# Top-k attention and a Fourier mixer on one core: the order of VectorE's top-k passes

## The chip, the cores and the metric

The kernel runs on one core of one Trainium2 chip. A core has five engines with a queue of instructions each, which run in order: TensorE (PE; its weight loads are listed apart as PEld), VectorE (DVE), ScalarE (ACT), GpSimd (POOL) and SyncE (SP), which here issues nearly all DMAs. They wait for one another, and for DMAs, through semaphores. The metric is the device time of one execution in microseconds; shown times are medians of several runs.

## What is computed

Two blocks follow one another. The first is attention in which each query keeps its 32 largest scores; the second mixes tokens and channels by a Fourier transform and puts an MLP behind it.

```python
def _attn_ref(q, k, v):                       # each (8, 8, 576, 64): batch, head, token, head_dim
    scores = scale * np.matmul(q, k.transpose(0, 1, 3, 2))
    kth = np.partition(scores, -top_k, axis=-1)[..., -top_k:-top_k + 1]      # top_k = 32
    scores = np.where(scores >= kth, scores, -1000000000.0)
    scores = scores - np.max(scores, axis=-1, keepdims=True)
    attn = np.exp(scores)
    attn = attn / (np.sum(attn, axis=-1, keepdims=True) + 1e-09)
    return np.matmul(attn, v)

def _moe_ref(x, w_ch1, w_ch2):                # x (8, 576, 512), weights 512 x 2048 and 2048 x 512
    mixed = np.real(np.fft.fft(np.fft.fft(x, axis=1), axis=2))
    u = x + mixed
    un = (u - mean(u)) / np.sqrt(var(u) + 1e-06)
    return u + np.maximum(un @ w_ch1, 0.0) @ w_ch2
```

The heads of a batch, side by side, are the second block's `x`. All is fp32.

## The kernel before

**Tiles.** Heads are taken in pairs, four pairs to a batch. The 576 queries of a pair of heads make nine tiles: four row blocks of 128 for each head, and one tile with the last 64 rows of both. So a batch has 36 tiles and the kernel 288, numbered 0 to 287. A tile is a matrix of 128 queries by 576 scores in the buffer `S` (six of them).

**Top-k on VectorE.** `top_ops` (L407) makes a tile's list of passes. A pass reads 576 scores per row. MAX8 (L425) writes the eight largest into `m`; MATCH_REPLACE8 (L427) writes a copy into `wk` in which these eight are replaced by a very small number. Four rounds of MAX8 with three MATCH_REPLACE8 between them leave the 32 largest in `m`, seven passes in all. The first round reads `S`, the others `wk`. A pass needs the one before it of its own tile: MATCH_REPLACE8 the eight values, the next MAX8 the changed copy. The program has a semaphore wait on VectorE itself for that, except at MAX8 on `S`.

A step `i` of the main loop (L1498) holds the last three passes of tile i, `first` (MAX8, MATCH_REPLACE8, MAX8), and the first four of tile i + 1, `second` (MAX8 on `S`, MATCH_REPLACE8, MAX8, MATCH_REPLACE8). L1611 to L1617 lay them down in turns. After the last pass of `first` the step puts in an integer shift on a weight chunk (`shift`, L200), in batch 0 alone. Behind the passes come small operations where there are some (`late_now` and the "dve" list): the reciprocal of the softmax sums (L591), the normalisation of a finished piece of `x` (L608, L615, from PSUM), statistics (L844), additions of finished products (L1008, L1121).

**What hangs on a tile's last pass.** The 1st and the 32nd of `m` become, on GpSimd, two biases `nt` (`bounds`, L434). ScalarE then makes `wk` from `S` with a steep relu (`mask`, L448), GpSimd subtracts it from `S` (L451), and ScalarE takes the exponential with the row sums (`expo`, L459). In batches 0 and 1 and for the last pair TensorE transposes the result (L527) and ScalarE copies it to `PT`. For the others (`by_dma`) ScalarE splits the words into two planes in `wk` (L472), SyncE sends them to DRAM (L485) and brings them back transposed (L506). TensorE multiplies `PT` with `v` (`attend`, L564). `wk` has three buffers for pairs of tiles and one for the tile of tails; one is free again when its planes are sent, or its transposes done.

**Where `S` comes from.** In step i TensorE makes the scores of tile i + 3 (L401, L386, the last 64 keys in L371), and ScalarE copies them to `S` (L404, L393, L375). ScalarE's queue has, in each step, the mask and the planes of earlier tiles first and these copies behind them.

**The rest of a step.** All queues are written in program order by a planner: it lays the transform of a finished batch (TensorE L755, L812, L816; its folds on GpSimd, or on VectorE for the first and the last batch) and the MLP's units (L966 hidden layer with the relu on ScalarE at L970; L993, L1032 and the products L1163 of the second layer) between the attention of the next batch. The last batch's MLP comes when no attention is left. Nothing is moved while it runs; an engine that comes to an instruction whose input is missing stands still.

Of the kernel before, what the change touches and what calls it, by code (L numbers as in the profile page):

```python
# [73 lines left out]
def kernel(  # L74
# [332 lines left out]
    def top_ops(i, rounds):  # L407

        if not 0 <= i < N:
            return []  # L410
        if i not in Wk:
            e = items[i][2]
            if e != 1:

                if e is None:
                    Wp[i] = attp.tile([P, 1, S], F32, name=f"wk_{i}", tag="W1", bufs=1)
                else:
                    Wp[i] = attp.tile([P, 2, S], F32, name=f"wk_{i}", tag="W", bufs=3)
            Wk[i] = Wp[i - 1][:, 1, :] if e == 1 else Wp[i][:, 0, :]
            M8[i] = small.tile([P, TOPK], F32, name=f"m8_{i}", tag="m8", bufs=5)  # L420
        w, m, s = Wk[i], M8[i], Ssb[i]
        ops = []
        for r in rounds:
            src, m8 = s if r == 0 else w, m[:, 8 * r:8 * r + 8]
            ops.append(lambda src=src, m8=m8: nc.vector.max(out=m8, in_=src))  # L425
            if r < TOPK // 8 - 1:
                ops.append(lambda src=src, m8=m8: nc.vector.match_replace(w, m8, src, NEG))  # L427
        return ops
# [955 lines left out]
    for b in range(B):  # L1384
        end = PER_BATCH * (b + 1) - 1
        last = b == B - 1
        first, soon = b == 0, b == 1
# [91 lines left out]
    def run(i, where):  # L1479
        for fn in plan.pop((i, where), []):  # L1480
            fn()
# [16 lines left out]
    while i < N + 5 or plan or queue or sums:  # L1498
# [111 lines left out]
                load_v(pair_of + 1)  # L1610
        first, second = top_ops(i, (2, 3)), top_ops(i + 1, (0, 1))  # L1611
        for n in range(max(len(first), len(second))):
            for ops in (first, second):
                if n < len(ops):
                    ops[n]()
                if ops is first and n == len(first) - 1:
                    run(i, "shift")  # L1617
# [56 lines left out]
```

## Time and profile before

| what | us |
|---|---|
| median of 3 runs (1851.18 to 1857.1) | 1854.34 |
| span of the profiled execution, first to last instruction | 1848.4 |
| TensorE busy (share of the span) | 1686.1 (91%) |
| VectorE busy | 1581.0 (86%) |
| ScalarE busy | 1294.9 (70%) |
| GpSimd busy | 919.5 (50%) |
| 864 MAX8 on `wk`, L425: busy, mean of one | 626.5, 0.749 |
| 288 MAX8 on `S`, L425 | 213.7, 0.742 |
| 576 MATCH_REPLACE8 on `wk`, L427 | 427.6, 0.742 |
| 288 MATCH_REPLACE8 on `S`, L427 | 213.6, 0.742 |

The span is one execution, the one that was profiled; the median is of other runs, timed without a profile. Top-k passes run from 10 us to 1641 us; what follows is the last batch's transform and MLP. Times in the timeline are microseconds from the span's start. Busy time is the union of the recorded lengths of an engine's instructions. A row of the waits names the waiting engine, tile and line, what it waited for, the total in us, how often and the longest. The chain of waits follows the work that ended last back from the end, at each step to what released it.

### The profile page before, as it was taken

The numbers are of one execution on the slowest core, as the hardware profiler recorded it, in microseconds if no ns is written. First come the engines' busy times: TensorE is split into PE (matmuls) and PEld (weight loads), VectorE is DVE, ScalarE is ACT, GpSimd is POOL, SyncE is SP. The second block draws the span as 40 slices with busy tenths as digits, with TensorE's granted clock in tenths as the row PEclk, the third lists the DMA queues.
The fourth block names the chain that finished last, engine by engine and source line by source line (L and its number), as shares of the span: only waits on it lengthen the run. The fifth ranks groups of instructions, "written<-read, shape, count | busy, mean of one in ns | idle before, by whom it ended". The sixth has DMA issues, their size and how long they took to land.

```text
span 1848.4 us, 26992 instructions
## 1 busy us (share of the span) xinstructions
PE 1686.1 (91%) x8134; PEld 1084.1 (59%) x8134; DVE 1581.0 (86%) x3301; ACT 1294.9 (70%) x3104; POOL 919.5 (50%) x1286
## 2 busy tenths in 40 slices
PE   5676699899898998999999999999999999999998
PEld 3344465374555655667565655666566756686677
DVE  7999989999899999999999999999999899944010
ACT  6878659687788778877787778777887678642100
POOL 4768744556634466356543565356634654350012
PEclk8878899899899999999999999999999999999999
DMA  5334016752558855577566855595566845520051
GB/s 168 107 92 118 20 44 178 189 137 59 127 135 200 214 133 131 134 207 179 117 149 166 222 127 127 137 249 145 137 144 181 199 104 140 152 80 7 6 174 57
DMA packets 513504, 249.16 MB, mean 135 GB/s; under 512 B 398288, under 2 KB 502352, under 8 KB 513360
## 3 DMA queue, kind: packets, MB, share of 16 engines
q1 hardware_dynamic: 511440, 243.04, 51.2%
q0 software_dynamic: 1152, 4.19, 0.7%
q8 instruction: 65, 1.06, 0.2%
q14 instruction: 79, 0.65, 0.1%
q10 hardware_dynamic: 768, 0.21, 0.0%
HBM read 93.63 MB, written 84.74 MB: 96 GB/s over the span
## 4 chain that ended last, share of the span: by engine, by line
PE 45%; DVE 27%; POOL 9%; issue 8%; ACT 7%; DMA 3%; SPq 0%; POOLq 0%; DVEq 0%; ACTq 0%
PE hp L966 16%; DVE wk L427 12%; DVE m L425 12%; PE cp L993 5%; PE o L564 5%; POOL wk L451 4%; PE sp L401 3%; PE cw L1163 3%; PE cv L1163 2%; ACT wk L448 2%; PE yp L755 2%; POOL fg L651 2%; PE cp L1032 2%; PE mp L816 1%; PE sp_t L371 1%
## 5 line engine op out<-in xcount | busy, mean ns | idle before, releaser
L451 POOL TENSOR_TENSOR wk<-S,wk 128x576 f32<-128x576 f32 x288 | 407.6, 1415 | 503.2 <-ACT wk L448 503.1
L425 DVE MAX8 m<-wk 128x8 f32<-128x576 f32 x864 | 626.5, 749 | 6.1
L966 PE MATMUL hp<-unT,w 128*128 128x256 f32 (+1 forms) x2048 | 525.1, 408 | 2.9 <-ACT hT L970 2.1
L966 PEld LDWEIGHTS hp<-unT,w 128*128 128x128 f32 x2048 | 379.5, 191 | 106.7 <-issue 9.9
L427 DVE MATCH_REPLACE8 wk<-m,wk 128x576 f32<-128x576 f32 x576 | 427.6, 742 | 0.0
L472 ACT COPY wk<-S 128x576 uint16<-128x576 uint16 x468 | 289.6, 670 | 0.0
L448 ACT ACTIVATE wk<-S,nt 128x576 f32<-128x576 f32 x288 | 223.5, 776 | 85.4 <-POOL nt L434 84.0
L993 PE MATMUL cp<-w,hT 128*128 128x512 f32 x512 | 232.6, 594 | 0.0
L970 ACT ACTIVATE hT<-hp 128x320 f32<-128x320 f32 (+1 forms) x256 | 103.7, 412 | 179.9 <-PE hp L966 178.2
L425 DVE MAX8 m<-S 128x8 f32<-128x576 f32 x288 | 213.7, 742 | 10.3 <-ACT S L375 10.2
L564 PE MATMUL o<-PT,v 128*64 128x256 f32 (+3 forms) x1440 | 198.7, 421 | 22.0 <-DMA PT<-planes 13.0
L427 DVE MATCH_REPLACE8 wk<-m,S 128x576 f32<-128x576 f32 x288 | 213.6, 742 | 0.0
L459 ACT ACTIVATE S<-wk,nt 128x576 f32<-128x576 f32 x234 | 184.3, 788 | 28.3 <-POOL wk L451 26.8
L401 PE MATMUL sp<-kT,qT 64*128 64x512 f32 (+1 forms) x528 | 168.9, 669 | 9.3 <-ACT means L1357 5.7
L564 PEld LDWEIGHTS o<-PT,v 128*64 128x64 f32 x1440 | 116.0, 155 | 97.8 <-issue 34.5
L404 ACT COPY S<-sp 128x512 f32<-128x512 f32 (+1 forms) x264 | 141.8, 588 | 32.5 <-PE sp L401 31.4
L993 PEld LDWEIGHTS cp<-w,hT 128*128 128x128 f32 x512 | 93.1, 191 | 89.2 <-issue 88.1
L1108 POOL TENSOR_TENSOR hT<-hT 128x512 f32<-128x512 f32 x64 | 81.2, 1275 | 117.8 <-ACT hT L970 87.9
L434 POOL TENSOR_TENSOR nt<-m,cc 128x2 f32<-128x2 f32 x288 | 59.9, 208 | 156.6 <-DVE m L425 154.3
L1163 PE MATMUL cw<-w,hT 128*128 128x256 f32 x448 | 104.9, 384 | 12.6 <-ACT ct L1133 10.2
L371 PEld LDWEIGHTS sp_t<-kt,qT 128*128 128x128 f32 x320 | 51.1, 194 | 102.3 <-issue 68.0
L1163 PEld LDWEIGHTS cw<-w,hT 128*128 128x128 f32 x448 | 82.6, 190 | 28.4 <-ACT ct L1133 12.6
(161 smaller groups left out, 2141.8 us busy)
## 6 DMA issues: line engine op xcount, KB each, us to landing
planes<-wk SPq DMA_DIRECT2D x208, 288.0 KB, 2.8
w<-w_parts SPq DMA_DIRECT2D x82, 512.0 KB, 5.0
space<-in_moe_w_ch_dram SPq DMA_DIRECT2D x32, 512.0 KB, 3.7
nat<-in_q_dram SPq DMA_DIRECT2D x128, 64.0 KB, 2.3
v<-in_v_dram SPq DMA_DIRECT2D x64, 128.0 KB, 3.0
out_dram<-x SPq DMA_DIRECT2D x32, 256.0 KB, 2.8
nat<-in_k_dram SPq DMA_DIRECT2D x62, 128.0 KB, 3.2
planes<-wk SPq DMA_DIRECT2D x52, 144.0 KB, 2.7
```

Source lines behind the costliest of these rows:

```text
L401: nc.tensor.matmul(sp[r], lhsT=qT[hd, q_cols], rhs=kT[hd, :], start=True, stop=True)
L404: nc.scalar.copy(out=s_t[r, keys], in_=sp[r])
L425: ops.append(lambda src=src, m8=m8: nc.vector.max(out=m8, in_=src))
L427: ops.append(lambda src=src, m8=m8: nc.vector.match_replace(w, m8, src, NEG))
L448: nc.scalar.activation(out=w, in_=Ssb[i], func=AF.Relu, scale=-FAR, bias=Nt[i][:, 1:2])
L451: nc.gpsimd.tensor_tensor(out=w, in0=Ssb[i], in1=w, op=ALU.subtract)
L459: nc.scalar.activation(out=Ssb[i] if by_dma(i) else w, in_=w, func=AF.Exp, bias=Nt.pop(i)[:, 0:1], accum_out=den_t[pair % 3][:, c:c + 1],)
L472: nc.scalar.copy(out=words[:, half, :], in_=src[:, half, :])
L564: nc.tensor.matmul(o[D * e:D * (e + 1), c0:c1], lhsT=vv[:, c, e, :], rhs=pt[:, NF if c == NF else (NF + 1) * e + c, c0:c1], start=(c == 0) ...
L966: nc.tensor.matmul(hp[:, 0:w], lhsT=w1[:, dt, P * it:P * (it + 1)], rhs=unT[:, dt, 0:w], start=(dt == 0), stop=(dt == NDT - 1),)
L993: nc.tensor.matmul(cp, lhsT=hT[:, it, P * n:P * (n + 1)], rhs=w2[:, it, :], start=(it == 0), stop=(it == NIT - 1),)
L1163: nc.tensor.matmul(dst, lhsT=h()[a][:, kc, :], rhs=rhs_of(kc), start=start and kc == 0, stop=kc == NK - 1, skip_group_check=True,)
```

## The change

The two lists of passes of a step are laid down in the other turn, the newer tile's first.

```diff
         first, second = top_ops(i, (2, 3)), top_ops(i + 1, (0, 1))
         for n in range(max(len(first), len(second))):
-            for ops in (first, second):
+            for ops in (second, first):
                 if n < len(ops):
                     ops[n]()
                 if ops is first and n == len(first) - 1:
                     run(i, "shift")
```

With F1 to F3 for the passes of `first` and S1 to S4 for those of `second`, VectorE's order in a step was, and becomes (the small operations stand behind the last pass in both):

```
before:  F1 S1 F2 S2 F3 (shift) S3 S4
after:   S1 F1 S2 F2 S3 F3 (shift) S4
```

F1 belongs to the tile of the S1 to S4 one step before. Tile 0's first four passes stand ahead of the loop, and the last tile's step has no `second`. Nothing else in the program is changed.

## The prediction

> **What bounds the kernel now.** The names first. In one step VectorE runs seven passes over 576 keys: F1, F2, F3 finish the older tile (MAX8, MATCH_REPLACE8, MAX8), S1 to S4 begin the newer one (MAX8 on `S`, MATCH_REPLACE8, MAX8, MATCH_REPLACE8). A MATCH_REPLACE8 shows as two rows, a short MATCH_VALUE_LOAD and the pass. I read VectorE's timeline first, one step without other work in it; columns are start, length, line and operation:
>
> ```profile
> 1156.08 0.74 DVE L427 MATCH_REPLACE8 wk<-m,wk 128x576 f32<-128x576 f32 x1
> 1156.85 0.76 DVE L425 MAX8 m<-wk 128x8 f32<-128x576 f32 x1
> 1157.53 0.74 DVE L425 MAX8 m<-S 128x8 f32<-128x576 f32 x1
> 1158.19 0.07 DVE L427 MATCH_VALUE_LOAD wk<-m,wk 128x8 f32 x1
> 1158.25 0.74 DVE L427 MATCH_REPLACE8 wk<-m,wk 128x576 f32<-128x576 f32 x1
> 1158.91 0.08 DVE L427 MATCH_VALUE_LOAD wk<-m,S 128x8 f32 x1
> 1158.98 0.74 DVE L427 MATCH_REPLACE8 wk<-m,S 128x576 f32<-128x576 f32 x1
> 1159.64 1.41 DVE L425 MAX8 m<-wk 128x8 f32<-128x576 f32 x2
> 1161.08 0.09 DVE L427 MATCH_VALUE_LOAD wk<-m,wk 128x8 f32 x1
> 1161.16 0.74 DVE L427 MATCH_REPLACE8 wk<-m,wk 128x576 f32<-128x576 f32 x1
> ```
>
> Read start to start, not by length. A pass that follows a pass of the other tile starts 0.66 to 0.67 us after it (1157.53 to 1158.19, 1158.25 to 1158.91, 1158.98 to 1159.64), which is before the 0.74 us of its forerunner are over. A pass that follows its own tile's starts later: F1 behind the S4 before it 1156.85 - 1156.08 = 0.77, and S4's load behind S3, which began 1159.64 + 0.67 = 1160.31, also 0.77. The reader sees two holds of 0.11 us per step.
>
> Then who waits for whom, VectorE up to the end of its top-k work (0 to 1640 us) and ScalarE in the second 200 us of the dense middle, and the chain of waits from 499 to 812 us; last the busy time by engine in two stretches (length, then PE, its weight loads, DVE, ACT, POOL, the granted clock, DMA share, GB/s):
>
> ```profile
> DVE x L608 <- PE tpx L604: 23.3, 10, 5.5
> DVE m L425 <- ACT S L375: 10.2, 7, 2.2
> DVE rd L591 <- ACT rd L590: 8.6, 6, 4.2
> ...
> DVE wk L427 <- DMA planes<-wk: 4.0, 2, 2.0
> ```
> ```profile
> ACT wk L448 <- POOL nt L434: 28.4, 17, 3.8
> ```
> ```profile
> by line: DVE wk L427 39.8%; DVE m L425 37.0%; issue 11.6%; DVE st L844 1.9%; ACT wk L472 1.9%; DVE x L608 1.2%; ACT wk L448 1.0%; POOL wk L451 0.9%; POOL hT L1108 0.8%; DVE x L1054 0.6%; DVE mv L845 0.6%; DVE x L615 0.6%; POOL nt L434 0.4%;
> ```
> ```profile
> 440.00:640.00 200.00, 182.34 (x873) 113.42 (x872) 188.58 (x390) 154.08 (x367) 102.00 (x149) 0.95 0.64 159
> 840.00:1040.00 200.00, 193.73 (x957) 123.69 (x955) 190.28 (x397) 156.07 (x373) 103.86 (x155) 1.00 0.65 161
> ```
>
> VectorE hardly ever waits: some 70 us in 1640, by the whole list. So where the chain lies on it, a shorter step is a shorter kernel. The chain in order of time has it there in batch 0 (9.5 to 194 us, but for excursions) and from 499 to 812 us, where L427, L425 and VectorE's small work are over four fifths; ScalarE waits there for the thresholds (17 times, 28.4 us), so TensorE is late for VectorE's sake. From 255 to 446 us and from 812 us on the chain is TensorE, GpSimd and ScalarE, but for stints of 3 to 8 steps, and TensorE is idle only 6 us of 200.
>
> **The change, part by part.** The build moves VectorE's rows alone: the order on TensorE, ScalarE, GpSimd and SyncE, DMA issues included, is the same, and so are all counts. The order becomes S1 F1 S2 F2 S3 F3 S4, then S1 of the next tile.
>
> *The holds.* No pass follows its own tile's any more. The new step, each gap from the row of an equal pair above: S1 to F1 0.67 (MAX8 to MAX8 of the other tile, F3 to S3), F1 to S2's load 0.66, its pass 0.06, F2's load 0.66, pass 0.07, S3 0.66, F3 0.67, S4's load 0.66, pass 0.06, next S1 0.66: 4.83 us. The old step is S1 at 1152.45 to S1 at 1157.53, 5.08. A pure step saves 0.25: two holds of 0.11 and 0.01 to 0.02 in each of two neighbours. Where a small operation (a normalisation, statistics, a late addition) stands between S4 and F1, only the hold at S3 and S4 goes: 0.11 + 0.02 = 0.13.
>
> The Trainium skill speaks against this: "VectorE: DVE Perf Modes", section "The DRAIN you can't avoid", holds that the next operation never starts before the pipeline is empty and that a semaphore between chained operations costs nothing extra, measured on eight copies. By it the saving would be 0 and the time, with F3 later, 1856. The rows above disagree, 0.66 against 0.77, and they decide.
>
> *The thresholds.* F3 goes from fifth to sixth place: 0.66 us later in its step, and with it `nt` (L434) on GpSimd, the mask (L448) on ScalarE, the subtraction (L451), and all that ScalarE has queued behind the mask: the copies of `S` for later tiles, relu evictions, the planes. It is paid once each time the chain leaves VectorE through F3, not in each step. Behind the mask lie 4 us of slack in the middle case of batches 4 to 6 (start of L448 minus end of F3, paired by tile), 0.3 to 2 in batch 2's second half.
>
> *The waits.* S1's wait for the `S` copies moves one place forward, S2's wait for a free `wk` buffer too; F1 or F2, and so F3, are now queued behind them. In most steps nothing is waited for: `S` is ready 7 to 9 us before S1 in the middle case. Where it is late, or the buffer is, F3 comes later than before, relative to that event. From a late S1 to the end of the F3 n steps on it was 5.08 n + 2.86 us (1157.53 to 1159.64 + 0.75) and becomes 4.83 n + 4.19 (0.67 + 0.66 + 0.06 + 0.66 + 0.07 + 0.66 + 0.67 + 0.74): 1.33 - 0.25 n more. From a late S2 it was 0.07 + 0.66 + 0.75 = 1.48 and becomes 2.86: 1.38 - 0.25 n. So a stretch between two such waits gains only if it has more than five steps.
>
> *The sum.* Batch 0 up to 194 us: 31 steps, 24 of them pure: 24 x 0.25 + 7 x 0.13 = 6.9, less 0.66 at the exit: 6.2 us. 499 to 812 us: 58 steps, 32 pure: 8.0 + 3.4 = 11.4, less 0.66: 10.7 us. Batch 1 (chain on TensorE): 0, between -1 and +4. Batches 4 to 7: stints of 3 and 7.5 steps, 1.38 - 0.25 x 3 = 0.6 lost and 0.25 x 7.5 - 1.38 = 0.5 won; I take 0 for each batch, with -3 (half of its 6 us of idle TensorE filled) and +1.5 (lost at two waits) as bounds. The tail after 1640 us is MLP on TensorE: 0. Together 16.9 us: the span of 1848.4 becomes 1831.5. The median of the runs, 1854.34, is 5.9 us above the span; I keep that difference: 1837.4, said as 1837.
>
> **Rivals.**
> 1. *TensorE takes it over.* For: TensorE is 97% busy from 840 us on and 91% already in 440 to 640. Then the 10.7 us are eaten by the first TensorE-bound stretch, batch 0's 6.2 remain: 1848. Against: ScalarE's 28.4 us of waits for thresholds, and TensorE idle 17.7 of 200 us there.
> 2. *More than counted.* VectorE saves 81 x 0.25 + 65 x 0.13 = 29 us in batches 4 to 7 as well, and half of TensorE's idle time closes: 3 us a batch, and 4 in batch 1: 1837 - 16 = 1821. Against: `S` comes within 0.3 us of S1 once or twice in each of these batches already, so VectorE will wait there.
> 3. *Slower: the old tile stuck behind the new one.* One mechanism, in batches 4 to 7 (145 steps): a faster VectorE runs into S1's wait at L425, F1 to F3 stand behind it, thresholds come later, ScalarE, whose queue holds the next `S` copies behind the mask, delivers them later still. Price 1.33 - 0.25 n per wait at intervals of n steps. At n = 3, 48 waits x 0.58 = +28 and the time 1865; it eats the 17 us won elsewhere from about n = 3.6. For: the wait moved is a true one. Against: in 0 to 1640 us VectorE waited for `S` 7 times, for anything 38 times in 288 steps, and where `S` is late the masks lag F3 by 4.7 to 11 us already.
> 4. *The change does not do what it says*: the hold belongs to something else, or a pass two places behind its own tile's is held as well. Then no gain and 2 x 0.66 lost: 1856. Against: F1 to F2 and S1 to S2 are two places apart today and run at 0.66.
>
> **How the numbers follow.** Forecast 0.57 (own range 1825 to 1845: batches 4 to 7 at -3 each, or at +1.5 each and three more exits at 0.66), rival 1 0.13, rival 2 0.15, rival 3 0.10, rival 4 0.05. What a measurement can tell from no change is 0.3%, 5.6 us: faster is below 1848.8, slower above 1859.9. Faster: the forecast, rival 2 and half of rival 1: 0.79; the same: the other half, rival 4 and the mild end of rival 3: 0.13; slower: 0.08. The range 1821 to 1851 takes in rivals 1 and 2 and leaves out what lies beyond.
>
> **What would show it.** Right: MATCH_REPLACE8 to MAX8 and MAX8 to load at 0.66 us everywhere, S1 to S1 at 4.83 in pure steps; S1 of tile 36 about 8 us earlier, and of tile 140 about 17; TensorE's busy time the same. ScalarE's waits for `nt` shrink between 499 and 812 us, and VectorE's own waits grow after 812. Wrong: 0.77 still there (rival 4); batches 4 to 7 longer than 201 us with L425 <- `S` at the head of VectorE's waits (rival 3); 499 to 812 not shorter although its steps are (rival 1).

## The result and the profile after

| | before | changed |
|---|---|---|
| median of the runs on the same chip (4 each), us | 1855.37 (1851.18 to 1857.1) | 1843.7 (1843.09 to 1844.21) |
| span of the profiled execution, us | 1848.4 | 1841.7 |

The ratio is 0.994 with a 95% interval of 0.9926 to 0.9954: faster by 0.6%, beyond the 0.3% that can be told from no change, but 6.7 us short of the 1837 forecast. The same kernel run 12 times more, beside 35 runs of the kernel before, gave 0.9955 (0.9937 to 0.9974). So the gain is 8 to 11 us where 16.9 were counted.

First the page of the changed kernel: the span, the busy time of the engines and the groups of top-k passes (busy time and mean ns of one; the last column is the engine's idle time before them and what ended most of it).

```profile
span 1841.7 us, 26992 instructions
PE 1683.0 (91%) x8134; PEld 1082.6 (59%) x8134; DVE 1540.8 (84%) x3301; ACT 1295.2 (70%) x3104; POOL 919.1 (50%) x1286
L425 DVE MAX8 m<-wk 128x8 f32<-128x576 f32 x864 | 618.5, 742 | 0.1
L425 DVE MAX8 m<-S 128x8 f32<-128x576 f32 x288 | 214.8, 746 | 18.5 <-ACT S L375 17.5
```

VectorE's busy time fell by 40.2 us (1581.0 to 1540.8), the span by 6.7. The mean of a MAX8 on `wk` hardly moved (749 to 742 ns): a hold lies between two starts, not in a length. One step of the changed kernel in VectorE's timeline, F1 to the next F1 (columns: start, length, line and operation):

```profile
1143.14 0.74 DVE L425 MAX8 m<-wk 128x8 f32<-128x576 f32 x1
1143.80 0.07 DVE L427 MATCH_VALUE_LOAD wk<-m,S 128x8 f32 x1
1143.86 0.74 DVE L427 MATCH_REPLACE8 wk<-m,S 128x576 f32<-128x576 f32 x1
1144.52 0.08 DVE L427 MATCH_VALUE_LOAD wk<-m,wk 128x8 f32 x1
1144.59 0.74 DVE L427 MATCH_REPLACE8 wk<-m,wk 128x576 f32<-128x576 f32 x1
1145.25 1.41 DVE L425 MAX8 m<-wk 128x8 f32<-128x576 f32 x2
1146.57 0.07 DVE L427 MATCH_VALUE_LOAD wk<-m,wk 128x8 f32 x1
1146.63 0.74 DVE L427 MATCH_REPLACE8 wk<-m,wk 128x576 f32<-128x576 f32 x1
1147.29 0.75 DVE L425 MAX8 m<-S 128x8 f32<-128x576 f32 x1
1147.96 0.74 DVE L425 MAX8 m<-wk 128x8 f32<-128x576 f32 x1
```

Every gap is 0.66 to 0.67 us and the step takes 1147.96 - 1143.14 = 4.82 us. Where S4 stood 0.77 behind S3, it now stands 1.32 behind the start of the pair S3 and F3 (1145.25 to 1146.57), two gaps of 0.66. Over all steps of batches 1 to 7 the median from S1 to S1 went from 5.08 or 5.09 to 4.82 or 4.83.

What became of it shows in the waits. VectorE, 0 to 1640 us (tile and line, what it waited for, total us, times, longest), then ScalarE's wait for the thresholds from 499 to 812 us, in the changed kernel, and last that wait in the kernel before:

```profile
DVE x L608 <- PE tpx L604: 32.0, 19, 6.2
DVE wk L427 <- DMA planes<-wk: 22.1, 4, 8.2
DVE rd L591 <- ACT rd L590: 21.4, 13, 3.6
DVE m L425 <- ACT S L375: 17.5, 11, 3.4
```
```profile
ACT wk L448 <- POOL nt L434: 23.5, 20, 4.0
```
```profile
ACT wk L448 <- POOL nt L434: 28.8, 22, 4.0
```

All four of VectorE's rows grew, from 46 us to 93 together; its waits up to 1640 us add to some 121 us, 68 before. ScalarE's wait for `nt` in that stretch shrank from 28.8 us to 23.5. The chain of waits by line, 499 to 812 us, has changed its head:

```profile
by line: PE hp L966 11.1%; issue 5.6%; DVE m L425 5.6%; POOL wk L451 4.6%; DVE wk L427 4.4%; PE o L564 4.2%; ACT wk L448 3.6%; ACT wk L472 3.4%; PE sp L401 2.4%; PE cw L1163 2.4%; ACT S L459 2.4%; PE cp L1032 2.3%; POOL fg L651 1.9%; PE cp 
```

L427 and L425 were 77% of it before and are 10% now; the MLP's matmuls on TensorE lead. Where the time was won is read best on TensorE, which runs the same instructions in the same order in all kernels here. The time between the same marked matmuls, in us:

```
stretch (times of before)          14-236      236-445     445-812     812-1640
before                             221.6       209.2       367.2       828.0
changed                            219.9       211.1       357.7       830.3
mean of the old order (profiles)   222.4 (4)   212.4 (7)   366.7 (6)   830.6 (7)
mean of the new order (profiles)   220.3 (6)   212.4 (7)   359.8 (8)   833.7 (6)
```

The last two rows take every profile of this study whose edit leaves that stretch in the one order or the other, without those with shifts or conversion left out where it is batch 0, and without the kernel that changes a wait in the last stretch. The kernel that moves F3 alone (below) counts as old, since its step is as long. In 445 to 812 us the two orders do not overlap (365.1 to 368.6 against 357.7 to 361.9). In 14 to 236 us they overlap a little (221.6 to 224.1 against 219.4 to 222.0), in 236 to 445 and 812 to 1640 us clearly.

Whole spans of single profiles decide nothing at this size: the changed kernel's second profile had a span of 1854.7 us, 13 us more than the first, and 35 runs of the kernel before lie between 1850.4 and 1864.7. Nor need a profiled execution be typical: that of the second profile was the slowest of its kernel's 12 runs, and so were, among theirs, those of four kernels below (batches 2 and 3 alone, batches 4 to 7 alone, shift behind the step, no shifts in the new order). So totals are compared by ratios over many runs below, and profiles by stretches.

### The profile page after: what moved, and what is told of

The parts are those of the page before. It is cut to its first block, busy times and chain, and to the rows that moved or that the text cites. A ratio compares the mean times of both kernels' runs of the same rounds, so it can differ in the third digit from the quotient of the medians.

```text
span 1841.7 us, 26992 instructions
## 1 busy us (share of the span) xinstructions
PE 1683.0 (91%) x8134; PEld 1082.6 (59%) x8134; DVE 1540.8 (84%) x3301; ACT 1295.2 (70%) x3104; POOL 919.1 (50%) x1286
## 4 chain that ended last, share of the span: by engine, by line
PE 45%; POOL 8%; ACT 6%; issue 5%; DMA 2%; DVE 2%; SPq 0%; POOLq 0%; DVEq 0%; ACTq 0%
PE hp L966 18%; PE o L564 4%; PE cw L1163 4%; PE cp L993 4%; POOL wk L451 4%; PE sp L401 3%; PE cv L1163 3%; PE cp L1032 2%; ACT wk L448 2%; POOL fg L651 2%; DMA PT<-planes 1%; PE mp L816 1%; PE sp_t L371 1%; ACT wk L472 1%; DVE m L425 1%
## 5 line engine op out<-in xcount | busy, mean ns | idle before, releaser
L425 DVE MAX8 m<-wk 128x8 f32<-128x576 f32 x864 | 618.5, 742 | 0.1
L427 DVE MATCH_REPLACE8 wk<-m,wk 128x576 f32<-128x576 f32 x576 | 425.9, 739 | 0.0
L425 DVE MAX8 m<-S 128x8 f32<-128x576 f32 x288 | 214.8, 746 | 18.5 <-ACT S L375 17.5
L564 PE MATMUL o<-PT,v 128*64 128x256 f32 (+3 forms) x1440 | 199.5, 422 | 24.5 <-DMA PT<-planes 19.7
L427 DVE MATCH_REPLACE8 wk<-m,S 128x576 f32<-128x576 f32 x288 | 213.0, 740 | 0.0
L459 ACT ACTIVATE S<-wk,nt 128x576 f32<-128x576 f32 x234 | 184.2, 787 | 24.5 <-POOL wk L451 23.3
L1163 PE MATMUL cw<-w,hT 128*128 128x256 f32 x448 | 105.6, 386 | 11.5 <-ACT ct L1133 10.2
```

Source lines behind the costliest of these rows:

```text
L459: nc.scalar.activation(out=Ssb[i] if by_dma(i) else w, in_=w, func=AF.Exp, bias=Nt.pop(i)[:, 0:1], accum_out=den_t[pair % 3][:, c:c + 1],)
L564: nc.tensor.matmul(o[D * e:D * (e + 1), c0:c1], lhsT=vv[:, c, e, :], rhs=pt[:, NF if c == NF else (NF + 1) * e + c, c0:c1], start=(c == 0) ...
L1163: nc.tensor.matmul(dst, lhsT=h()[a][:, kc, :], rhs=rhs_of(kc), start=start and kc == 0, stop=kc == NK - 1, skip_group_check=True,)
```

## The experiments

All edits are to the loop shown in the change, unless a line says otherwise. Ratios are to the kernel before, run on the same chip. A ratio's distance from 1, times its 1857 us, is given as us.

| kernel | ratio (95% interval), runs | us |
|---|---|---|
| changed kernel again | 0.9955 (0.9937 to 0.9974), 12 | -8.4 |
| new order in batch 0 alone | 0.9982 (0.9968 to 0.9996), 12 | -3.3 |
| new order in batches 2 and 3 alone | 0.997 (0.9954 to 0.9985), 12 | -5.6 |
| new order in batches 4 to 7 alone | 0.9997 (0.9982 to 1.0012), 12 | -0.6 |
| new order in batches 0 to 3 | 0.9944 (0.993 to 0.9958), 6 | -10.4 |
| new order, old at the late `wk` buffer | 0.9945 (0.993 to 0.996), 6 | -10.2 |
| new order, shift behind the step | 0.9933 (0.9915 to 0.9952), 6 | -12.4 |
| no shifts, old order | 0.9962 (0.9946 to 0.9978), 5 | -7.1 |
| no shifts, new order | 0.9908 (0.9891 to 0.9926), 6 | -17.1 |
| no conversion, old order | 0.9949 (0.9931 to 0.9968), 4 | -9.5 |
| no conversion, new order | 0.9938 (0.9923 to 0.9953), 4 | -11.5 |
| F3 one place later, holds kept | 1.001 (0.9998 to 1.0022), 10 | +1.9 |

### The change in parts

The changed kernel once more, and the new order in one group of batches at a time.

> The changed kernel once more, for a closer interval and a second profile. The hold theory in the prediction's sizes: 17 us below the kernel before. From the two traces so far (span 6.7 us shorter, medians 11.7 us apart, the kernel before between 1851 and 1857 from run to run): 8 to 12 us below.

```diff
-            for ops in (first, second):
+            for ops in (second, first) if i < PER_BATCH else (first, second):
```

> New order in the steps of batch 0 alone. If VectorE's own passes bound batch 0, as predicted: 6 us below the kernel before. The rival, that the weight shift (L200) now stands behind GpSimd's two-input operations and gives most of it back: VectorE's 36 steps shorten by 3 us, not 8, the 32 shifts take some 5 us more in sum, and the time is 0 to 2 us lower.

```diff
+            for ops in (second, first) if 2 * PER_BATCH <= i < 4 * PER_BATCH else (first, second):
```

> New order in batches 2 and 3 alone (tiles 72 to 143). Hold theory: 9 to 11 us below the kernel before, nearly all of what the change brings. Rival (TensorE takes it over behind tile 144): under 3 us.

```diff
+            for ops in (second, first) if i >= 4 * PER_BATCH else (first, second):
```

> New order in batches 4 to 7 alone. Predicted: 0, at most 1.5 us a batch lost. If the older tile stuck behind S2's wait for a wk buffer (third step of each batch) is what costs time: 2 to 4 us above the kernel before, TensorE's waits for PT at L564 longer in batches 5 and 7. Rival of more gain: 3 us a batch below.

The three parts add to -9.5 us, the whole measured -8.4 and, at first, -11.1. So the gain is made in batch 0 and in batches 2 and 3, and batches 4 to 7 are worth -0.6 us, with an interval of -3.3 to +2.2. The first two parts lie between what was expected and its rival: 3.3 us between 6 and 0 to 2, and 5.6 between 9 to 11 and under 3. In batch 0 the signs of the rival came: from S1 of tile 0 to S1 of tile 36 VectorE took 2.7 us less than before, and the shifts 5.6 us more. Turning batches 2 and 3 shows in its own stretch of TensorE alone: 445 to 812 us take 359.3, with batch 0 or the late batches turned 365.7 and 365.2.

A later kernel takes the new order in batches 0 to 3 and the old behind them, to see whether the late ones lose.

```diff
+            for ops in (second, first) if i < 4 * PER_BATCH else (first, second):
```

> New order in batches 0 to 3, the old one from tile 144 on. From the parts (batch 0 alone 3.7 us, batches 2 and 3 alone 5.2, batches 4 to 7 alone 0.9 below the kernel before): 8 to 11 us below. If the new order costs time in the late batches, this beats the changed kernel by 1 to 4 us; if not, no difference.

(The 3.7, 5.2 and 0.9 us are differences of medians; the table goes by ratios.) 0.9944 against the whole change's 0.9955, with intervals that overlap. The late stretch of TensorE took 832.6 us with the old order here and 837.1 with the new one in the late batches alone, but 830.3 in the first profile of the whole change. Much of this goes with TensorE's granted clock. In this stretch it stood at half for 13.7 us in the two longest profiles, both of the new order (837.1 and 836.4), and for 6.8 us in the one of 830.3. At 10.2 us of half clock three profiles of the old order took 832.0 to 832.6 us and two of the new 832.1 and 832.7; at 6.8 us it is 830.3 against 830.3 and 833.3. So a loss hardly shows at an equal clock. Whether the new order brings more time at half clock, and the late batches lose up to 3 us by it, stays open.

### Is it the holds, or F3's place?

```diff
-            for ops in (first, second):
+            for ops in (first, second) if n < 2 else (second, first):
```

> Order F1 S1 F2 S2 S3 F3 S4: F3 in sixth place as in the changed kernel, but of the two holds only that at S3 and S4 gone, 0.13 us a step; the one at S4 and F1 stays. If the holds make the gain: about half of it, 3 to 6 us below the kernel before, pure steps of 4.95 us. If something else in the new order makes it (S1 first): nothing, or F3's later place costs 1 to 2 us.

The order becomes F1 S1 F2 S2 S3 F3 S4. The expectation overlooked that S3 now stands behind S2 of its own tile. VectorE's timeline of this kernel in a step of batch 2:

```profile
563.41 0.74 DVE L427 MATCH_REPLACE8 wk<-m,wk 128x576 f32<-128x576 f32 x1
564.07 0.08 DVE L427 MATCH_VALUE_LOAD wk<-m,S 128x8 f32 x1
564.14 0.74 DVE L427 MATCH_REPLACE8 wk<-m,S 128x576 f32<-128x576 f32 x1
564.91 1.42 DVE L425 MAX8 m<-wk 128x8 f32<-128x576 f32 x2
566.25 0.07 DVE L427 MATCH_VALUE_LOAD wk<-m,wk 128x8 f32 x1
```

S2 starts at 564.14 and S3 at 564.91, 0.77 later: the hold between S3 and S4 has moved to S2 and S3. In the kernel before, F3 followed S2 with the same operations at 0.66 (1158.98 to 1159.64); here S4's load follows F3 at 0.66 (the pair starts at 564.91, F3 some 0.68 later, the load at 566.25). So the hold goes with the tile, not with the kind of operation. The pure step is 5.08 us as before. That makes the kernel a control: F3 stands in sixth place as in the changed kernel, and both holds are still there. It is no faster (1.001, 0.9998 to 1.0022), and 445 to 812 us take 368.6 us of TensorE. F3's later place alone, then, gains nothing and costs between nothing and 4 us. The kernel also lacks S1's first place, so it does not part the holds from that. That the holds make the gain is inferred: S1's place could only save waiting, and VectorE's waits grew (68 to 121 us), while the step shrank by 0.26 us (5.086 to 4.822, median of batches 1 to 7), where the two holds and their neighbours were counted at 0.25.

### Batch 0: what holds it

Before, VectorE had a single wait from 20 to 236 us:

```profile
DVE w L200 <- ACT w L192: 1.8, 1, 1.8
```

It was to gain 6.9 us up to 194 us, and about 8 by S1 of tile 36. From S1 of tile 0 to S1 of tile 36 it took 203.3 us before and 200.0 after: 3.3. The rest went into the shifts. Pairs of rows from the two timelines: the shift on VectorE, and the two-input GpSimd operation beside it; the kernel before, then the changed one:

```profile
180.87 1.09 DVE L200 TENSOR_SCALAR w<-w 128x512 int32<-128x512 int32 x1
...
180.40 1.28 POOL L221 TENSOR_TENSOR w<-w,space 128x512 f32<-128x512 f32 x1
```
```profile
179.09 1.42 DVE L200 TENSOR_SCALAR w<-w 128x512 int32<-128x512 int32 x1
...
178.94 1.29 POOL L221 TENSOR_TENSOR w<-w,space 128x512 f32<-128x512 f32 x1
```

The median shift took 0.41 us before. Both long ones end 0.28 us behind the end of the operation beside them (181.96 and 181.68; 180.51 and 180.23), so the earlier one falls into it, the longer it is. All shifts of 0.5 us and more in these two profiles end 0.28 or 0.29 us behind a two-input GpSimd operation over 512 or 576 words a row. The 32 shifts together took 17.6 us before and 22.2 after (23.7 in the changed kernel's second profile; 19.6 and 19.1 in two others with the old order in batch 0). Of the 8 us, 4.6 went there. Two edits test it: the shift put behind the step, and the shifts left out.

```diff
-                if ops is first and n == len(first) - 1:
-                    run(i, "shift")
+        if first:
+            run(i, "shift")
```

> The new order with batch 0's weight shift (L200) behind S4 instead of behind F3. If the shift's wait for GpSimd's two-input operations eats batch 0's saving: the 32 shifts sum to 13 to 16 us instead of 22 to 24, batch 0 is 3 to 5 us shorter. Rival (GpSimd, whose join L219 waits for the shift and now gets it a pass later, is the bound of batch 0): batch 0 the same or longer.

The shifts still took 21.9 us there, and 14 to 236 us took 219.8 of TensorE against 219.9: moving them by one pass does not take them away from GpSimd's operations. The expectation fell.

```diff
-                    run(i, "shift")
+                    plan.pop((i, "shift"), None)
```

> The old order, the weight shifts of batch 0 left out (the output is not the reference's). Base for the next run: batch 0 shorter by the shifts, 15 to 18 us of VectorE, 10 or more in all if VectorE bounds it; 1840 to 1848.

> The new order, the weight shifts of batch 0 left out. If the shift is what keeps batch 0 from gaining: TensorE's batch 0 6 to 8 us shorter than in the old order without shifts (2 with shifts). If ScalarE or GpSimd bound it: 0 to 3 us shorter again.

Busy time in 20 to 236 us (length, then PE, its weight loads, DVE, ACT, POOL, the granted clock, DMA share, GB/s) and VectorE's wait for `S` in it; no shifts, the old order and then the new:

```profile
20.00:236.00 216.00, 146.56 (x731) 90.51 (x733) 201.96 (x421) 175.87 (x414) 153.31 (x162) 0.78 0.32 90
```
```profile
DVE m L425 <- ACT S L375: 8.5, 8, 3.9
```
```profile
20.00:236.00 216.00, 144.37 (x735) 89.53 (x737) 195.64 (x421) 176.32 (x415) 153.46 (x162) 0.79 0.32 90
```
```profile
DVE m L425 <- ACT S L375: 15.5, 10, 4.8
```

VectorE's work shrinks by 6.3 us, as counted, and all of it reappears as waiting for `S`: 7.0 us more. On TensorE 14 to 236 us take 218.2 and 217.9. Leaving the shifts out was to shorten batch 0 by 10 us or more and brought 3.4. I had expected the full gain of the holds here, 6 to 8 us, and that fell too. So these two profiles show a second limit in batch 0 at about 218 us, 3.4 below the 221.6 of the kernel before; by them VectorE bounds the batch, but only by that much. Single profiles of one order differ by up to 2.6 us in this stretch, so the size is rough. By total time the pair differs by more, 7.1 against 17.1 us. The profiled execution of the new order took 1850.5 us, and the median of its six runs is 1842.8, so its stretches do not show where the others gained, and batch 0 may be among them: this is open.

What sets 218 us? The next pair leaves out the rest of the weights' conversion (the lines for "convert", "shift", "join" and "pool" in the plan), which is work of ScalarE, VectorE and GpSimd in batch 0.

```diff
-        at(s0 + 1, "convert", lambda n=n: rest(n))
-        at(s0 + 1, "shift", lambda n=n: shift(n))
-        at(s0 + 1, "join", lambda n=n: join(n, 0))
-        at(s0 + 1, "pool", lambda n=n: join(n, 1))
```

> The old order with batch 0's weight conversion cut to its first step: two ScalarE operations, the VectorE shift and two GpSimd operations on each of 32 chunks are left out (the output is not the reference's). Base for the next run. If ScalarE and GpSimd, and not VectorE, set batch 0's pace, it is 20 us or more shorter than the 218 to 222 us seen so far.

> The new order with the same operations left out. If batch 0 gains little from the order because ScalarE and GpSimd set its pace, then with them relieved VectorE sets it and the order brings 6 to 8 us in batch 0 (0 to 2 with the conversion in). If the order brings nothing in batch 0 for another reason (F3's later place, TensorE): 0 to 2 us again.

The limit falls to 212 us, not by the 20 us or more that were expected if ScalarE and GpSimd set the pace, and again the order brings nothing: 212.0 old, 212.7 new, where the new one was expected 6 to 8 us ahead. VectorE's wait for `S` from 20 to 236 us rises from 3.9 to 12.2 us. VectorE is still busy 205.5 of 216 us in the old order. GpSimd and ScalarE have slack. The row of the window without conversion, old order, and from its chain of waits in order of time (start, us, what) one round:

```profile
20.00:236.00 216.00, 148.95 (x781) 94.19 (x782) 205.54 (x429) 145.07 (x358) 73.73 (x99) 0.79 0.32 91
```
```profile
129.25 1.41 POOL wk L451
130.66 0.02 issue
130.69 0.88 ACT wk L459 x2
131.56 0.04 issue
131.61 0.67 PE tpP L527 x4
132.28 0.02 issue
132.30 0.58 ACT PT L530
132.89 0.68 ACT wk L448
133.57 0.07 issue
133.64 1.42 POOL wk L451
```

ScalarE is busy 145 of 216 us and GpSimd 74, yet one hands over to the other without a gap: GpSimd subtracts, ScalarE takes the exponential, TensorE transposes, ScalarE copies and then masks the next tile, GpSimd subtracts again. (TensorE transposes in batch 0, and after it only for the last pair of batch 1 and the very last pair; the rest of batch 1 already goes through DRAM.) The round takes 4.39 us (129.25 to 133.64) and has no VectorE in it. It cannot set the pace of the whole batch alone: from S1 of tile 0 to S1 of tile 36 both kernels take 190.6 us, 5.3 us a tile. So what sets the limit stays open. What the runs show is the limit itself, that VectorE then waits for `S`, and that less work on VectorE, ScalarE and GpSimd does not let the new order through. F3's later place, with the copies of `S` queued behind the mask on ScalarE, is a rival that none of these runs excludes.

### The late `wk` buffer

Where S2 waits for a free `wk` (the third tile of each of batches 4 to 7, in the second step), F2, S3 and F3 are now queued behind it. The kernel before, the changed kernel and one with the old order in just these steps, in VectorE's timeline in batch 5:

```profile
1034.46 0.09 DVE L427 MATCH_VALUE_LOAD wk<-m,S 128x8 f32 x1 [2.00 <-POOL wk L451]
```
```profile
1018.75 0.74 DVE L425 MAX8 m<-wk 128x8 f32<-128x576 f32 x1
1024.63 0.09 DVE L427 MATCH_VALUE_LOAD wk<-m,S 128x8 f32 x1 [5.14 <-DMA planes<-wk]
1024.71 0.74 DVE L427 MATCH_REPLACE8 wk<-m,S 128x576 f32<-128x576 f32 x1
1025.37 0.08 DVE L427 MATCH_VALUE_LOAD wk<-m,wk 128x8 f32 x1
1025.43 0.74 DVE L427 MATCH_REPLACE8 wk<-m,wk 128x576 f32<-128x576 f32 x1
1026.09 1.41 DVE L425 MAX8 m<-wk 128x8 f32<-128x576 f32 x2
```
```profile
1026.96 0.09 DVE L427 MATCH_VALUE_LOAD wk<-m,S 128x8 f32 x1 [3.52 <-DMA planes<-wk]
1027.04 0.74 DVE L427 MATCH_REPLACE8 wk<-m,S 128x576 f32<-128x576 f32 x1
1027.70 1.41 DVE L425 MAX8 m<-wk 128x8 f32<-128x576 f32 x2
```

```diff
+            for ops in (second, first) if i < 4 * PER_BATCH or i % PER_BATCH != 1 else (first, second):
```

> The new order everywhere but in the second step of batches 4 to 7, where the next tile's S2 waits for its wk buffer; there the old order, so that F1 and F2 (and F3 after one pass) stand ahead of that wait. If F1 to F3 stuck behind it cost the late batches their time: 2 to 5 us below the changed kernel, so 10 to 12 below the kernel before, and VectorE's F3 of tile 181 ends some 4 us earlier relative to the start of the load that waits. Rival (that loss is spread over many steps, or is run-to-run noise): no change, 7 to 8 us below the kernel before.

VectorE reaches the wait earlier and stands longer, 5.14 us against 2.00. From the load to F3 it is 1026.09 + 0.67 - 1024.63 = 2.13 us in the new order and 0.74 in the old: 1.39 apart, where the prediction had 1.38. The expectation of 4 us was wrong. The kernel's ratio, 0.9945, cannot be told from the change's 0.9955, so this wait has no price that these runs could see.

No version clearly beats the changed kernel: of those that leave nothing out, the one with the shift behind the step has the lowest ratio, 0.9933, and its interval overlaps with those of the changed kernel's two measurements.

## Why the prediction was right, and where it was short

Right in direction, 6.7 us short of the time by the first four runs. By the 12 later ones (median 1849.35, by the ratio 8.4 us below the kernel before) the gain is half of what was forecast, so that the first four came as near as they did is in part luck. Step by step:

- **The holds: right in mechanism and size.** A pass behind its own tile's started 0.777 us after it, in the changed kernel one behind the other tile's starts after 0.659 to 0.668; the pure step was said to be 4.83 us and is 4.82 to 4.83. The rule of the Trainium skill that was weighed ("VectorE: DVE Perf Modes", section "The DRAIN you can't avoid") says that a semaphore between chained operations costs nothing extra, measured there on eight copies; for these passes the rows show 0.11 to 0.12 us. The same section says that an operation which is not held starts earlier, and that agrees: 0.66 us start to start at a recorded length of 0.74. The prediction left that sentence out when it took the page to forbid any saving. The kernel with F3 moved and the holds kept (1.001) shows that F3's place is not the gain, and the step shrank by what the holds are worth. Rival 4 is out.
- **499 to 812 us: right place, mis-sized term.** The steps were to save 11.4 us there. From S1 of tile 72 to S1 of tile 144 VectorE took 395.5 us before and 383.7 after, 11.8 less; by the means of five profiles of the old order and eight of the new it is 8.4 (395.0 to 386.6). VectorE's waits from 425 to 812 us rose, from 8.7 us to 12.4, and to 16.1 in the second profile. The term of the sum was -10.7 and measured -6.9 on TensorE (445 to 812 us) and -5.6 in the run of that part alone. What failed is the step from VectorE's saving to the end. TensorE stood idle 27.9 to 28.9 us of this stretch in the old order and still 22.9 to 24.5 in the new: only some 5 us of idle time belonged to VectorE (the other 2 of the 6.9 lie in TensorE's busy time), and the chain now runs over TensorE's MLP. Rival 1 was half right, for this stretch.
- **Batch 0: the failed step.** "31 steps" times the saving, 6.2 us, took for granted that nothing lies just beneath VectorE. It measured -2 us on TensorE and -3.3 by the run of that part alone. The pair without shifts puts the next limit roughly 3.4 us below, what sets it is open, and shifts drawn out beside GpSimd took 4.6 of VectorE's 8 us back. The chain of waits had VectorE there with good reason: VectorE waited for 1.8 us of 216. A chain names the engine that is last, not by how much.
- **Batch 1: 0 forecast**, and 236 to 445 us take TensorE 212.4 us in the mean of either order.
- **Batches 4 to 7: 0 forecast, -0.6 measured**, and its interval (-3.3 to +2.2) lies inside the bounds that were given (-12 to +6). S2's wait is as described, 1.39 against 1.38. Rival 3, the old tile stuck behind the new one, did not come: VectorE's wait for `S` from 812 to 1640 us rose from 8.9 us to 15.1, 4 times to 8, not 48. Rival 2 did not come either: VectorE's saving turned into its waits.
- **F3's later place** was priced at two exits of 0.66 us; the control allows -0.4 to +4.1.
- **The time around the span.** 5.9 us were kept between span and median. A run lies 1.8 us above its own span (1843.5 against 1841.7, and 1856.47 against 1854.7 for the second profile); the other 4.1 were chance, since the profiled execution of before was one of its shortest. That is no error of the sum, but it shows what one execution is worth here.

The signs that were named came in kind: ScalarE's wait for `nt` shrank, VectorE's waits grew. S1 of tile 140 is 11.5 us earlier (797.3 to 785.8), not 17; S1 of tile 36 is 3.4 earlier (213.2 to 209.8), not 8.

## What to carry to other kernels

Where two independent chains share VectorE, lay them so that no operation follows its own forerunner, and read start to start to see whether it pays. Before multiplying such a saving by the steps on the chain, ask how far beneath the next limit lies: one run that takes the engine's other work away shows that limit. And compare programs stretch by stretch between the same instructions when the runs of one program spread more than the effect.

## What the runs showed that was not expected

- **A clock that comes and goes.** TensorE's granted clock drops to half in stretches that are multiples of 3.41 us. Up to 230 us it stood at half for 88.7 us in the profile of before and 99.0 in the changed kernel's, and from 440 to 840 us for 23.9 and 13.7. Where a stretch falls differs between runs of one program. By an estimate each single one costs at most 1.7 us, half its length; the spread of the spans is partly this. The Trainium skill ("TensorE: Matmul & The Clock Gate", Part 1) gives a free-running window of about 3.4 us for it, which agrees with the 3.41.
- **VectorE's shift waits for GpSimd.** A 128x512 int32 shift of 0.41 us took up to 1.42 us and ended 0.28 us behind a two-input GpSimd operation that ran beside it. So a faster order on VectorE can run into its neighbour's work and lose there part of what it won.
